# Attention with a mixture of depths: the column of router scores by a diagonal select, in four of eight batches

## The chip, the cores and the metric

The kernel runs on one core of one Trainium2 chip. The metric is the device time of one launch in microseconds. Before the change the median of 3 runs is 205.4 us (205.3 to 205.61). PE is TensorE, DVE is VectorE, ACT is ScalarE, POOL is GpSimd and SP is SyncE.

## The reference

Squared-ReLU attention over 8 batches of 12 heads (448 tokens, 64 columns a head), and then in each batch the 128 tokens with the highest router score go through a two-layer MLP.

```python
# attention, batch 8, heads 12, seq 448, head_dim 64
scores = scale * np.matmul(q, k.transpose(0, 1, 3, 2))
attn = np.maximum(scores, 0.0) ** 2 / S
attn_out = np.matmul(attn, v)
x = attn_out.transpose(0, 2, 1, 3).reshape(B, S, H * D)          # 8 x 448 x 768
# mixture of depths, F = 1024, capacity 128
scores = np.einsum('bsd,d->bs', x, w_gate)
out = x.copy()
for b in range(B):
    top_idx = np.argpartition(-scores[b], capacity)[:capacity]
    xe = x[b, top_idx]
    h = np.maximum(xe @ w1, 0.0)
    ye = h @ w2
    g = 1.0 / (1.0 + np.exp(-scores[b, top_idx]))
    out[b, top_idx] = x[b, top_idx] + g[:, None] * ye
```

## The kernel before

The order of all work is written out by hand: one string of items, `ORDER`, is walked from front to back, and each item issues its instructions. Every engine takes its own instructions in that order and waits only for semaphores. An item is a name and numbers, then the PSUM bank (`at`) and, for an eviction, the engine (`A` for ACT, `D` for DVE). There are 8 PSUM banks, and items share them by number.

Attention goes by units of 4 heads: unit u belongs to batch u // 3, so there are 24. `T` and `TE` transpose q and k on PE and copy them to `qkt` (line 279 on DVE). `S,u,c` makes a block of scores of key group c (0 to 6) in two banks (line 247), `R,u,c` evicts it with a ReLU into `r_sb` (line 275 on ACT, 277 on DVE), `Q,u,g` squares a group of such blocks on DVE into `a_sb` (line 260). The groups are c = 0, 1; c = 2, 3; c = 4, 5, 6. `V,u,c` multiplies block c with v (line 268), so `V,u,2` waits for `Q,u,1`. `X` evicts the result as xT, and `RT`, `RE` turn it into rows of tokens, `x_sb`.

The router follows a batch's last unit. `G` makes the row of scores on PE, with the gate vector spread over all 128 columns, so that every partition of the bank holds the same row of 448 scores. `bc` copies this to `bc_sb` (128 x 512 fp32, line 275 on ACT). The same scores are also needed as a column, one per partition, in 4 groups of 128 tokens: `col` (line 343) makes it by four fp32 PE transposes of partition 0's row with a 1 x 1 identity, into a bank, and `colE` (line 349, DVE) copies the 128 x 4 result into `x_sb` beside the tokens (`cols`). `rk` (line 359, DVE) compares row and column, into the 0/1 tile `mk` and partial ranks; `cs` adds `mk` up on PE, `ri` (line 382, DVE) makes ranks. `sc` scatters token rows by rank to DRAM (line 386, issued from POOL), `rb` reads the first 128 back as `xe` (SP). Then `ix`, `xt` and `xtE` (xeT), `h` and `hE` (first layer), `y` and `yE` (second layer, `orow`), and `ADD` (line 514, POOL) writes them back.

POOL also issues every load of q, k, v and the weights (`Lq`, `Lk`, `Lv`, `W1`, `W2`: lines 108 to 124) and every store of plain rows (`ST`, line 313). `mk` and `bc_sb` have two buffers each, by the parity of the batch. `tie` is a constant mask made by POOL selects near the start (line 180).

Of the kernel before, what the change touches and what calls it, by code (L numbers as in the profile page):

```python
# [23 lines left out]
def kernel(  # L24
# [559 lines left out]
    S,18,5,0 S,17,5,2 R,18,5,0,A yE,2,1,4 y,2,0,2,5 R,17,5,2,A y,2,0,4,5 y,2,0,6,5 sc,3,1 S,17,6,0 col,4,4  # L584
    V,15,0,6 S,18,0,2 ST,2,1 V,15,1,6 V,15,2,6 R,17,6,0,A yE,2,0,5 Q,17,0 V,15,3,6 S,19,0,0 V,15,4,6 sc,3,0
    colE,4,4 R,18,0,2,A sc,3,2 V,15,5,6 V,15,6,6 S,18,2,2 V,17,0,4 R,19,0,0,A V,17,1,4 V,17,2,4 X,15,6,A
    V,17,3,4 Q,17,2 S,18,1,0 V,17,4,4 R,18,2,2,D V,17,5,4 V,17,6,4 V,16,0,6 V,16,1,6 R,18,1,0,A ST,2,0 V,16,2,6
    X,17,4,A S,18,3,2 Lv,6,0,6 V,16,3,6 S,18,4,0 R,18,3,2,A V,16,4,6 ADD,2 V,16,5,6 V,16,6,6 rk,4,0 rk,4,1
    rk,4,3 Lq,7,0,6 R,18,4,0,D T,20,4,0 Lk,7,0,6 X,16,6,A rb,3 T,20,4,1 S,18,6,2 S,19,6,0 rk,4,2 G,5,0,6
    R,18,6,2,A G,5,1,6 TE,20,4,2,D G,5,2,6 R,19,6,0,A xt,3,4 S,19,1,2 ST,3,1 Q,18,0 S,19,5,0 bc,5,6,A R,19,1,2,A  # L590
    ix,3 xtE,3,4,D Q,18,2 RT,17,5 R,19,5,0,A cs,4,4 RT,16,6 ri,4,4 RE,16,6,A col,5,7 S,19,4,2 S,19,2,0 Q,19,0
    R,19,2,0,A h,3,0,4 h,3,1,4 h,3,2,4 colE,5,7 V,18,0,6 Q,18,1 S,19,3,0 R,19,4,2,A V,18,1,6 RE,17,5,D V,18,2,6
    V,18,3,6 S,20,5,2 R,19,3,0,A V,18,4,6 rk,5,0 V,18,5,6 V,18,6,6 R,20,5,2,A S,20,0,0 R,20,0,0,A h,3,3,4
    h,3,4,5 hE,3,0,4,A Q,19,2 h,3,5,5 h,3,6,5 sc,4,2 S,20,4,0 rk,5,3 S,20,3,2 y,3,1,0,4 X,18,6,A Q,19,1 h,3,7,5
    T,21,6,0 T,21,6,1 R,20,4,0,A R,20,3,2,D hE,3,1,5,A S,20,2,0 S,20,1,2 y,3,1,2,4 TE,21,6,2,D sc,4,1 RT,15,5
    sig,3 R,20,2,0,A V,19,0,6 S,21,4,0 V,19,1,6 R,20,1,2,A rk,5,2 V,19,2,6 sc,4,0 V,19,3,6 rk,5,1 V,19,4,6
    RE,15,5,D sc,4,3 V,19,5,6 R,21,4,0,A V,19,6,6 X,19,6,A S,20,6,2 S,21,1,0 ST,4,1 cs,5,5 Q,20,1 y,3,1,4,4
    ri,5,5 ST,3,0 T,22,6,0 T,22,6,1 R,21,1,0,A Q,20,0 R,20,6,2,A S,21,6,0 R,21,6,0,A y,3,0,0,5 TE,22,6,2,D
    y,3,1,6,4 y,3,0,2,5 Q,20,2 y,3,0,4,5 S,22,0,2 S,21,0,0 V,20,0,6 R,22,0,2,A V,20,1,6 V,20,2,6 yE,3,1,4
    R,21,0,0,A V,20,3,6 V,20,4,6 rb,4 V,20,5,6 S,21,2,2 R,21,2,2,A Lv,7,0,6 V,20,6,6 sc,5,2 RT,18,4 y,3,0,6,5  # L600
    X,20,6,D yE,3,0,5 S,21,3,0 Q,21,0 S,22,6,2 T,23,6,0 RE,18,4,A T,23,6,1 sc,5,0 G,6,0,5 R,21,3,0,A G,6,1,5
    R,22,6,2,A G,6,2,5 xt,4,4 bc,6,5,A TE,23,6,2,D S,22,1,2 S,22,2,0 col,6,5 ix,4 xtE,4,4,D h,4,4,7 colE,6,5
    RT,20,4 R,22,1,2,A rk,6,1 h,4,5,7 R,22,2,0,A rk,6,2 rk,6,0 RT,19,5 sig,4 sc,5,1 S,22,3,2 RE,20,4,A RE,19,5,D
    S,21,5,0 h,4,6,7 rk,6,3 h,4,7,7 cs,6,4 sc,5,3 R,21,5,0,A h,4,0,5 h,4,1,5 hE,4,1,7,A R,22,3,2,A Q,21,1
    h,4,2,5 h,4,3,5 ADD,3 S,22,4,0 S,23,2,2 V,21,0,6 hE,4,0,5,A V,21,1,6 ri,6,4 R,23,2,2,A V,21,2,6 Q,21,2
    V,21,3,6 V,21,4,6 V,21,5,6 V,21,6,6 R,22,4,0,D S,22,5,0 R,22,5,0,A S,23,3,2 R,23,3,2,A Q,22,1 y,4,1,0,4
    y,4,1,2,4 y,4,0,0,5 Q,22,0 y,4,1,4,4 X,21,6,A y,4,1,6,4 S,23,4,0 R,23,4,0,A S,23,0,2 ST,4,0 y,4,0,2,5 Zl
    y,4,0,4,5 rb,5 y,4,0,6,5 RT,21,6 xt,5,7 Q,22,2 S,23,1,0 sc,6,0 R,23,0,2,A S,23,5,2 sc,6,3 yE,4,1,4 yE,4,0,5
    RE,21,6,D V,22,0,4 V,22,1,4 ix,5 xtE,5,7,D V,22,2,4 V,22,3,4 Q,23,1 V,22,4,4 V,22,5,4 R,23,1,0,A sc,6,2
    V,22,6,4 S,23,6,0 h,5,4,7 R,23,5,2,A sc,6,1 h,5,0,6 R,23,6,0,A h,5,1,6 Q,23,0 h,5,2,6 h,5,3,6 X,22,4,A  # L610
    h,5,5,7 V,23,0,2 Q,23,2 V,23,1,2 hE,5,0,6,D V,23,2,2 V,23,3,2 V,23,4,2 V,23,5,2 V,23,6,2 ADD,4 G,7,0,6
    RT,22,5 h,5,6,7 G,7,1,6 ST,6,0 X,23,2,A RE,22,5,A G,7,2,6 bc,7,6,A h,5,7,7 RT,23,1 ST,6,1 y,5,0,0,4
    hE,5,1,7,A RE,23,1,A col,7,6 y,5,0,2,4 rb,6 colE,7,6 rk,7,0 y,5,1,0,6 y,5,1,2,6 y,5,1,4,6 y,5,0,4,4
    y,5,0,6,4 rk,7,1 hot,7,1 hot,7,0 y,5,1,6,6 xt,6,7 rk,7,3 sig,5 xg,7,0,0 xg,7,1,0 rk,7,2 hot,7,2 hot,7,3
    xg,7,2,0 xg,7,3,0 ix,6 xtE,6,7,A h,6,0,5 ST,5,0 xgE,7,1,0,A yE,5,1,6 yE,5,0,4 h,6,1,5 h,6,2,5 h,6,3,5
    h,6,4,2 xgE,7,0,0,A h,6,5,2 hE,6,0,5,A p,7,0 p,7,1 h,6,6,2 p,7,2 p,7,3 sel,7,7 ST,5,1 ST,7,0,0,512
    ST,7,1,0,512 ST,7,0,512,768 ST,7,1,512,768 h,6,7,2 sE,7,0,7 sE,7,1,-1 sE,7,2,-1 sgl,7 y,6,1,0,0 y,6,1,2,0
# [56 lines left out]
```

## Time and profile before

| | |
|---|---|
| median of 3 runs | 205.4 us (205.3 to 205.61) |
| the profiled execution's own time | 204.92 us |
| its span, first to last instruction | 203.2 us |
| granted TensorE clock, mean | 0.999 |
| busy: PE, PE weight loads | 188.6 us (93%), 120.9 us (59%) |
| busy: DVE, ACT, POOL | 173.2 us (85%), 166.6 us (82%), 108.9 us (54%) |

Three engines are near full at the same time. A busy share is a mean over the launch, so it doesn't say which of the three sets the pace in a stretch; that is read from the idle time in front of an instruction and from what ended it. Starts are in microseconds from the span's start, and two rows of one engine overlap a little: the distance between two starts is what an instruction takes of its engine, the duration includes its tail.

### The profile page before, as it was taken

Reading aid. Unit: us, or ns where it says so; the run is one execution under the profiler, and the core shown is the slowest. Engines: PE = TensorE matmul, PEld = TensorE weight load, DVE = VectorE, ACT = ScalarE, POOL = GpSimd, SP = SyncE. Lnnn points to the kernel's source line nnn. Section 1 sums busy time; section 2 is a strip of 40 time slices with the busy share of each in tenths; the row PEclk is TensorE's granted clock in tenths of the full one; section 3 lists DMA queues with packets and bytes.
Section 4 is the critical chain, followed back from the end, with each engine's and each line's share of the span. In section 5 each row is a group of like instructions: output and inputs, shape, how many; then the busy total and the mean of one; then the engine's idle time right before and its main releaser. Section 6 shows DMA issues by size and latency. Waiting matters only on the chain.

```text
span 203.2 us, 6985 instructions
## 1 busy us (share of the span) xinstructions
PE 188.6 (93%) x3028; PEld 120.9 (59%) x3028; DVE 173.2 (85%) x274; ACT 166.6 (82%) x216; POOL 108.9 (54%) x133
## 2 busy tenths in 40 slices
...
GB/s 185 180 203 202 205 204 204 206 214 121 16 92 220 206 211 151 280 219 230 52 338 203 125 65 221 222 231 183 210 301 175 130 162 18 75 391 412 175 65 155
DMA packets 28970, 37.89 MB, mean 186 GB/s; under 512 B 2523, under 2 KB 23813, under 8 KB 28940
## 3 DMA queue, kind: packets, MB, share of 16 engines
...
q8 instruction: 23, 0.38, 0.7%
...
## 4 chain that ended last, share of the span: by engine, by line
PE 60%; ACT 25%; issue 6%; DVE 4%; DMA 2%; POOL 1%; POOLq 1%; ACTq 0%; DVEq 0%
PE banks L215 34%; ACT r_sb L275 23%; PE banks L247 14%; PE banks L268 11%; DMA kf<-in_k_dram 2%; ACT xT_sb L275 2%; DVE mk L359 1%; PE banks L343 1%; POOLq L669 1%; DVE qkt L279 1%; DVE a_sb L260 1%; PE banks L154 1%; POOL q_sb L478 1%; POOL out_dram L514 0%; ACT bc_sb L275 0%
## 5 line engine op out<-in xcount | busy, mean ns | idle before, releaser
L275 ACT ACTIVATE r_sb<-banks 128x896 bf16<-128x896 f32 x155 | 132.9, 950 | 12.1 <-PE banks L247 9.4
L260 DVE TENSOR_TENSOR a_sb<-r_sb 128x1792 bf16<-128x1792 bf16 (+1 forms) x72 | 87.4, 1238 | 0.3 <-ACT r_sb L275 0.2
L386 POOL DMA_INDIRECT xe_dram<-x_sb,rank_i x28 | 41.4, 1478 | 51.5 <-DVE rank_i L382 37.8
L247 PE MATMUL banks<-qkt 64*64 64x448 bf16 x672 | 58.4, 363 | 6.5 <-ACT r_sb L275 4.8
L268 PE MATMUL banks<-a_sb,v_sb 64*64 64x448 bf16 x672 | 43.6, 351 | 0.0
L247 PEld LDWEIGHTS <-qkt 64*64 64x64 bf16 x672 | 22.6, 104 | 29.6 <-issue 18.3
L279 DVE COPY qkt<-banks 128x1792 bf16<-128x1792 bf16 (+1 forms) x25 | 26.2, 1050 | 4.8 <-PE banks L215 3.4
L268 PEld LDWEIGHTS <-v_sb 64*64 64x64 bf16 x672 | 21.1, 106 | 9.5 <-issue 1.2
L215 PE MATMUL banks<-xeT,w_sb 128*128 128x128 bf16 x384 | 25.4, 219 | 0.5 <-DVE xeT L279 0.5
L514 POOL DMA_INDIRECT out_dram<-orow,idx x7 | 10.8, 1540 | 27.0 <-DVE orow L509 16.3
L215 PE MATMUL banks<-w_sb,hT 128*128 128x384 bf16 x128 | 24.6, 327 | 0.2 <-DVE hT L277 0.2
L215 PEld LDWEIGHTS <-w_sb 128*128 128x128 bf16 x384 | 22.0, 98 | 4.0 <-issue 3.4
L275 ACT ACTIVATE xT_sb<-banks 128x896 bf16<-128x896 f32 x19 | 18.0, 948 | 2.4 <-PE banks L268 2.4
L277 DVE TENSOR_SCALAR r_sb<-banks 128x896 bf16<-128x896 f32 x13 | 14.1, 1088 | 3.8 <-PE banks L247 2.4
L215 PEld LDWEIGHTS <-hT 128*128 128x128 bf16 x128 | 10.9, 98 | 10.3 <-issue 3.6
L359 DVE SCALAR_TENSOR_TENSOR mk<-bc_sb,x_sb,tie 128x448 bf16<-128x448 f32 (+4 forms) x32 | 15.2, 501 | 0.2
L215 PE MATMUL banks<-ident,xT_sb 128*128 128x128 bf16 x192 | 14.8, 220 | 0.2 <-ACT xT_sb L275 0.2
L215 PE MATMUL banks<-ident,k_sb 128*64 128x128 bf16 x336 | 14.0, 221 | 0.2 <-ACT k_sb L275 0.2
L215 PE MATMUL banks<-ident,q_sb 128*64 128x128 bf16 x336 | 14.0, 222 | 0.1
L215 PEld LDWEIGHTS <-xT_sb 128*128 128x128 bf16 x192 | 11.4, 98 | 4.2 <-issue 2.5
L215 PEld LDWEIGHTS <-q_sb 128*64 128x64 bf16 x336 | 10.3, 109 | 5.8 <-issue 5.0
L313 POOL DMA_DIRECT2D out_dram<-x_sb x18 | 12.1, 679 | 2.1 <-ACT x_sb L275 1.4
...
## 6 DMA issues: line engine op xcount, KB each, us to landing
...
```

The lines of the kernel that those rows point to most:

```text
L154: nc.tensor.matmul(out=banks[col:col + 64, at + x, :S], lhsT=zero[lo:lo + 64, 0:64], rhs=zero[lo:lo + 64, :], start=True, stop=True, skip_ ...
L215: nc.tensor.matmul(out=out, lhsT=lhsT, rhs=rhs, start=start, stop=stop, skip_group_check=True, **kw)
L247: nc.tensor.matmul(out=banks[col:col + 64, at + x, :S], lhsT=sb[lo:lo + 64, 1, c, hh, :], rhs=sb[lo:lo + 64, 0, :, hh, :], start=True, sto ...
L260: nc.vector.tensor_tensor(out=a, in0=r, in1=r, op=ALU.mult)
L268: nc.tensor.matmul(out=banks[col:col + 64, at + x, :S], lhsT=vs[lo:lo + 64, 2 * i + x, c, :], rhs=a[lo:lo + 64, c - SLOTS[g][0], x, :], st ...
L275: nc.scalar.activation(out=out_, in_=in_, func=func or AF.Copy, scale=scale)
L277: nc.vector.tensor_scalar(out=out_, in0=in_, scalar1=0.0, scalar2=None, op0=ALU.max)
L279: nc.vector.tensor_copy(out=out_, in_=in_)
L313: nc.gpsimd.dma_start(out=rows, in_=x_rows[b % NROW][64 * cp:64 * cp + 64, 0:NJ - cp, c0:c1])
L359: nc.vector.scalar_tensor_tensor(out=dst, in0=self.bc_[:n, t0:S], scalar=self.cols[:n, j:j + 1], in1=tie[:n, j, t0:], op0=ALU.subtract, op ...
L386: done = nc.gpsimd.indirect_dma_start(out=xe_dram[self.b][:, :], out_offset=bass.IndirectOffsetOnAxis(ap=self.rank_i[:, j:j + 1], axis=0), ...
L514: done = nc.gpsimd.indirect_dma_start(out=out[0:self.b + 1].rearrange("b s d -> (b s) d"), out_offset=bass.IndirectOffsetOnAxis(ap=self.id ...
```

## The change

In batches 2, 3, 4 and 5, `col` and `colE` give way to `dg` and `dgE`; batches 0, 1, 6 and 7 keep them. `dg` is one POOL select that reads all of `bc_sb` as 4 blocks of 128, keeps in each block the element whose place equals the partition's number, and writes zero elsewhere: 128 x 512 fp32 into the memory of the batch's `mk` tile, which `rk` overwrites afterwards. `dgE` is a DVE sum over each block of 128, which leaves the column in `cols`. No PSUM bank is used. `dg` stands behind `bc` (in batch 4 later, behind the loads `Lv,6`), `dgE` where `colE` stood (in batch 4 later, in front of the first `rk`).

```diff
+        def dg(self):
+            self.own_ = f32(mk_sb[self.b % 2])[:, :NJ * 128].rearrange("p (j t) -> p j t", j=NJ)
+            nc.gpsimd.affine_select(
+                out=self.own_, in_=self.bc_.rearrange("p (j t) -> p j t", j=NJ),
+                compare_op=ALU.is_equal, fill=0.0, base=0, pattern=[[0, NJ], [-1, 128]],
+                channel_multiplier=1)
+
+        def dgE(self):
+            nc.vector.tensor_reduce(out=self.cols, in_=self.own_, axis=mybir.AxisListType.X,
+                                    op=ALU.add)
...
-    S,10,5,2 rk,1,3 bc,2,5,A R,10,5,2,A T,11,6,0 xt,0,5 R,10,2,0,A T,11,6,1 RE,7,4,D rk,1,1 ix,0 xtE,0,5,D
+    S,10,5,2 rk,1,3 bc,2,5,A dg,2 R,10,5,2,A T,11,6,0 xt,0,5 R,10,2,0,A T,11,6,1 RE,7,4,D rk,1,1 ix,0 xtE,0,5,D
...
```

DVE in batches 3 to 4, from the second-layer evictions of batch 2 to the `TE` of unit 20; `x_sb_93` holds the column of batch 4, `a_sb` rows are `Q`. Before:

```order
L509 SCALAR_TENSOR_TENSOR orow<-banks,g__2503,xe 128x384 x2
L260 TENSOR_TENSOR a_sb_2718<-r_sb_2624 128x1792
L349 COPY x_sb_93<-banks 128x4
L260 TENSOR_TENSOR a_sb_2772<-r_sb_2567 128x2688
L277 TENSOR_SCALAR r_sb_2782<-banks 128x896
L359 SCALAR_TENSOR_TENSOR mk_97,rank_f_99<-bc_sb_95,x_sb_93,tie 128x448
```

And now:

```order
L521 SCALAR_TENSOR_TENSOR orow<-banks,g__2497,xe 128x384 x2
L260 TENSOR_TENSOR a_sb_2708<-r_sb_2618 128x1792
L260 TENSOR_TENSOR a_sb_2761<-r_sb_2561 128x2688
L277 TENSOR_SCALAR r_sb_2771<-banks 128x896
L357 TENSOR_REDUCE x_sb_93<-mk_97 128x4
L371 SCALAR_TENSOR_TENSOR mk_97,rank_f_99<-bc_sb_95,x_sb_93,tie 128x448
```

The column moves two instructions back, behind `Q,17,2` and `R,18,2`, and reads `mk` instead of a bank.

DVE in batch 5, from xeT to the square `Q,18,1` (`a_sb_2985`, now `a_sb_2973`) and what follows it. Before:

```order
L279 COPY xeT<-banks 128x768
L260 TENSOR_TENSOR a_sb_2917<-r_sb_2677 128x2688
L382 TENSOR_TENSOR rank_i<-rank_f_99,banks 128x4
L260 TENSOR_TENSOR a_sb_2958<-r_sb_2757 128x1792
L349 COPY x_sb_94<-banks 128x4
L260 TENSOR_TENSOR a_sb_2985<-r_sb_2782 128x1792
L279 COPY x_sb_94<-banks 128x4x256
```

And now:

```order
L279 COPY xeT<-banks 128x768
L260 TENSOR_TENSOR a_sb_2909<-r_sb_2671 128x2688
L394 TENSOR_TENSOR rank_i<-rank_f_99,banks 128x4
L260 TENSOR_TENSOR a_sb_2946<-r_sb_2746 128x1792
L357 TENSOR_REDUCE x_sb_94<-mk_98 128x4
L260 TENSOR_TENSOR a_sb_2973<-r_sb_2771 128x1792
L279 COPY x_sb_94<-banks 128x4x256
```

Here the sum stands exactly where the copy stood, directly in front of `Q,18,1`.

POOL in batch 2, from the loads of k and v to the scatters of batch 1 and the stores behind them; `w_sb` is the load `W2`. Before:

```order
L111 DMA k_sb_85<-in_k_dram 128x6x448
L115 DMA v_sb_87<-in_v_dram 128x3x448
L118 DMA v_sb_87<-in_v_dram 64x3x448 x2
L124 DMA w_sb<-in_moe_w_dram 128x8x768
L386 DMA xe_dram_103<-x_sb_93,rank_i 128x386 x4
```

And now:

```order
L111 DMA k_sb_85<-in_k_dram 128x6x448
L115 DMA v_sb_87<-in_v_dram 128x3x448
L118 DMA v_sb_87<-in_v_dram 64x3x448 x2
L351 AFFINE_SELECT mk_97<-bc_sb_95 128x512
L124 DMA w_sb<-in_moe_w_dram 128x8x768
L398 DMA xe_dram_103<-x_sb_93,rank_i 128x386 x4
```

The select stands in front of `W2`, whose issue is therefore behind `bc,2`.

## Rows read from the trace of the kernel before

**Rows 1.** The page's first part: busy us, share of the span, instructions.

```profile
PE 188.6 (93%) x3028; PEld 120.9 (59%) x3028; DVE 173.2 (85%) x274; ACT 166.6 (82%) x216; POOL 108.9 (54%) x133
```

**Rows 2.** The page's chain that ended last, by engine, share of the span.

```profile
PE 60%; ACT 25%; issue 6%; DVE 4%; DMA 2%; POOL 1%; POOLq 1%; ACTq 0%; DVEq 0%
```

**Rows 3.** The chain in order of time at `col,2`: start, us, what.

```profile
72.73 0.34 PE banks L343 x4
```

**Rows 4.** Timelines of ACT and DVE, batch 2: start, us, what, idle before, releaser.

```profile
70.11 4.40 ACT L275 ACTIVATE r_sb<-banks 128x896 bf16<-128x896 f32 x5
75.00 3.35 ACT L275 ACTIVATE r_sb<-banks 128x896 bf16<-128x896 f32 x4 [0.49 <-ACT r_sb L275]
...
79.42 1.09 DVE L277 TENSOR_SCALAR r_sb<-banks 128x896 bf16<-128x896 f32 x1 [1.04 <-PE banks L215]
```

**Rows 5.** Timeline of all engines, batch 3.

```profile
92.52 0.55 ACT L275 ACTIVATE bc_sb<-banks 128x448 f32<-128x448 f32 x1
...
94.96 0.49 PE L215 MATMUL banks<-xeT,w_sb 128*128 128x128 bf16 x6 [0.51 <-DVE xeT L279]
...
98.26 0.92 ACT L275 ACTIVATE r_sb<-banks 128x896 bf16<-128x896 f32 x1 [1.52 <-PE banks L247]
...
99.18 1.09 DVE L277 TENSOR_SCALAR r_sb<-banks 128x896 bf16<-128x896 f32 x1 [1.14 <-PE banks L247]
```

**Rows 6.** DVE's timeline through batches 4 and 5.

```profile
127.32 1.09 DVE L279 COPY qkt<-banks 128x1792 bf16<-128x1792 bf16 x1 [0.36 <-PE banks L215]
...
130.50 0.16 DVE L349 COPY x_sb<-banks 128x4 f32<-128x4 f32 x1
130.57 1.55 DVE L260 TENSOR_TENSOR a_sb<-r_sb 128x2688 bf16<-128x2688 bf16 x1
132.04 1.08 DVE L277 TENSOR_SCALAR r_sb<-banks 128x896 bf16<-128x896 f32 x1
133.04 0.68 DVE L359 SCALAR_TENSOR_TENSOR mk<-bc_sb,x_sb,tie 128x448 bf16<-128x448 f32 x1
...
133.64 0.55 DVE L359 SCALAR_TENSOR_TENSOR mk<-bc_sb,x_sb,tie 128x320 bf16<-128x320 f32 x1
...
140.90 1.08 DVE L260 TENSOR_TENSOR a_sb<-r_sb 128x1792 bf16<-128x1792 bf16 x1
141.90 0.69 DVE L279 COPY x_sb<-banks 128x1024 bf16<-128x1024 bf16 x1
```

**Rows 7.** Timeline of PE's weight loads at `V,18,2`.

```profile
142.04 0.14 PEld L268 LDWEIGHTS <-v_sb 64*64 64x64 bf16 x7 [0.15 <-issue]
```

**Rows 8.** Timeline around `W2`: ACT's `bc,2`, POOL's `W2`, PE's first `y`.

```profile
60.15 0.97 POOL L124 DMA_DIRECT2D w_sb<-in_moe_w_dram x1
...
67.82 0.54 ACT L275 ACTIVATE bc_sb<-banks 128x448 f32<-128x448 f32 x1
...
83.39 1.47 PE L215 MATMUL banks<-w_sb,hT 128*128 128x384 bf16 x8
```

**Rows 9.** Stretches: us, busy by engine, clock, DMA share, GB/s.

```profile
62.00:64.00 2.00, 1.92 (x44) 1.18 (x39) 2.00 (x3) 2.00 (x3) 0.00 (x0) 1.00 1.23 231
...
78.00:80.00 2.00, 2.00 (x37) 1.53 (x36) 0.96 (x2) 2.00 (x4) 1.93 (x3) 1.00 0.19 62
```

**Rows 10.** POOL's selects of `tie` at line 180: duration min/median/max in ns.

```profile
L180 POOL TENSOR_SCALAR_AFFINE_SELECT tie<-tie x4: 553/1062/1417, 20.7 to 28.4; 128x448 bf16<-128x448 bf16 x4
```

**Rows 11.** DVE and POOL at the longest of these selects, timelines of each.

```profile
23.11 2.08 DVE L260 TENSOR_TENSOR a_sb<-r_sb 128x1792 bf16<-128x1792 bf16 x2
24.19 1.42 POOL L180 TENSOR_SCALAR_AFFINE_SELECT tie<-tie 128x448 bf16<-128x448 bf16 x1
```

**Rows 12.** POOL's and ACT's timeline in front of the selects of batches 4 and 5.

```profile
127.81 1.31 POOL L118 DMA_DIRECT2D v_sb<-in_v_dram x2
...
137.62 0.55 ACT L275 ACTIVATE bc_sb<-banks 128x448 f32<-128x448 f32 x1
```

More of the change, by code (lines that the diff above doesn't have):

```diff
@@ L566 @@
     S,13,6,0 T,14,6,0 X,11,4,A T,14,6,1 R,13,6,0,D cs,2,4 R,13,5,2,A S,12,0,0 Lv,4,0,6 TE,14,6,2,D Q,12,2 ADD,0
-    S,12,1,2 R,12,0,0,A rb,1 R,12,1,2,A G,3,0,5 G,3,1,5 G,3,2,5 xt,1,6 Q,12,0 S,14,3,0 bc,3,5,A ri,2,4 S,13,0,2
-    sc,2,3 RT,11,5 sig,1 sc,2,1 col,3,7 ix,1 xtE,1,6,D R,14,3,0,A S,14,2,0 R,13,0,2,A h,1,4,4 colE,3,7 rk,3,0
+    S,12,1,2 R,12,0,0,A rb,1 R,12,1,2,A G,3,0,5 G,3,1,5 G,3,2,5 xt,1,6 Q,12,0 S,14,3,0 bc,3,5,A dg,3 ri,2,4
+    S,13,0,2 sc,2,3 RT,11,5 sig,1 sc,2,1 ix,1 xtE,1,6,D R,14,3,0,A S,14,2,0 R,13,0,2,A h,1,4,4 dgE,3 rk,3,0
     S,13,3,2 R,14,2,0,A RT,10,6 rk,3,3 sc,2,2 R,13,3,2,A S,13,4,0 R,13,4,0,A h,1,5,4 RE,11,5,D h,1,0,5 h,1,6,4
@@ L583 @@
     R,17,1,0,A y,2,1,2,4 T,19,6,0 Q,17,1 R,17,0,2,A y,2,0,0,5 y,2,1,4,4 Q,16,2 y,2,1,6,4 T,19,6,1 TE,19,6,2,D
[L584 to L617, printed above, removed]
@@ L618 @@
-    ADD,5 xr,7 hE,6,1,2,D y,6,1,4,0 y,6,1,6,0 sig,6 h,7,0,4 h,7,4,1 yE,6,1,0 h,7,5,1 h,7,1,4 h,7,2,4 h,7,3,4
-    h,7,6,1 h,7,7,1 hE,7,0,4,D hE,7,1,1,A y,6,0,0,6 y,6,0,2,6 y,6,0,4,6 y,6,0,6,6 yE,6,0,6 ADD,6 y,7,1,0,2
-    y,7,0,0,4 y,7,0,2,4 y,7,1,2,2 y,7,0,4,4 y,7,0,6,4 y,7,1,4,2 yE,7,0,4 y,7,1,6,2 yE,7,1,2 ADD,7
+    S,18,5,0 S,17,5,2 R,18,5,0,A yE,2,1,4 y,2,0,2,5 R,17,5,2,A y,2,0,4,5 y,2,0,6,5 sc,3,1 S,17,6,0 V,15,0,6
+    S,18,0,2 ST,2,1 V,15,1,6 V,15,2,6 R,17,6,0,A yE,2,0,5 Q,17,0 V,15,3,6 S,19,0,0 V,15,4,6 sc,3,0 R,18,0,2,A
@@ new lines @@
+    sc,3,2 V,15,5,6 V,15,6,6 S,18,2,2 V,17,0,4 R,19,0,0,A V,17,1,4 V,17,2,4 X,15,6,A V,17,3,4 Q,17,2 S,18,1,0
+    V,17,4,4 R,18,2,2,D V,17,5,4 V,17,6,4 V,16,0,6 V,16,1,6 R,18,1,0,A ST,2,0 V,16,2,6 X,17,4,A S,18,3,2
+    Lv,6,0,6 dg,4 V,16,3,6 S,18,4,0 R,18,3,2,A V,16,4,6 ADD,2 V,16,5,6 V,16,6,6 dgE,4 rk,4,0 rk,4,1 rk,4,3
+    Lq,7,0,6 R,18,4,0,D T,20,4,0 Lk,7,0,6 X,16,6,A rb,3 T,20,4,1 S,18,6,2 S,19,6,0 rk,4,2 G,5,0,6 R,18,6,2,A
+    G,5,1,6 TE,20,4,2,D G,5,2,6 R,19,6,0,A xt,3,4 S,19,1,2 ST,3,1 Q,18,0 S,19,5,0 bc,5,6,A dg,5 R,19,1,2,A ix,3
@@ new lines @@
+    xtE,3,4,D Q,18,2 RT,17,5 R,19,5,0,A cs,4,4 RT,16,6 ri,4,4 RE,16,6,A S,19,4,2 S,19,2,0 Q,19,0 R,19,2,0,A
+    h,3,0,4 h,3,1,4 h,3,2,4 dgE,5 V,18,0,6 Q,18,1 S,19,3,0 R,19,4,2,A V,18,1,6 RE,17,5,D V,18,2,6 V,18,3,6
+    S,20,5,2 R,19,3,0,A V,18,4,6 rk,5,0 V,18,5,6 V,18,6,6 R,20,5,2,A S,20,0,0 R,20,0,0,A h,3,3,4 h,3,4,5
+    hE,3,0,4,A Q,19,2 h,3,5,5 h,3,6,5 sc,4,2 S,20,4,0 rk,5,3 S,20,3,2 y,3,1,0,4 X,18,6,A Q,19,1 h,3,7,5 T,21,6,0
+    T,21,6,1 R,20,4,0,A R,20,3,2,D hE,3,1,5,A S,20,2,0 S,20,1,2 y,3,1,2,4 TE,21,6,2,D sc,4,1 RT,15,5 sig,3
```

31 lines of the change are left out of this document (28 added, 3 removed).

## The prediction

> **What bounds the kernel now.** I read the busy shares first, then the chain of waits, then the timelines at the four places that the change touches. The shares alone decide nothing: PE has 188.6 us of work in a span of 203.2 us, but DVE has 173.2 us [rows 1], and DVE is idle at the start and the end, so in the middle it can be as full as PE. The chain puts 60% of the span on PE and only 4% on DVE [rows 2]. By this view the change takes work from the engine that sets the end and gives work to two that don't. The reader should keep in mind what a chain can't show: it names the engine that came last, and not by how little the next one came earlier. That margin is read from the idle time in front of instructions, place by place.
>
> Two places have idle time on DVE, and one has none. Behind batch 2's column DVE waits 1.04 us for PE at 79.42 us [rows 4]. Behind batch 3's it waits 1.14 us at 99.18 us, and ACT 1.52 us at 98.26 us [rows 5]. In batches 4 and 5 DVE works without a gap worth naming from 127.32 to 141.90 us [rows 6]; the wait in front of 127.32 us was for PE. In this stretch DVE is a full queue, started by PE and then running by itself.
>
> **What goes.** Each of the four changed columns takes four fp32 transposes off PE, 0.34 us a column in the chain in order of time [rows 3]; batches 4 and 5 have a piece as long there, and batch 3's transposes stand inside a wait. Four columns make 4 x 0.34 = 1.36 us of PE, which is the most that the change can give back. It also takes four copies off DVE. They last 0.16 us, but the next instruction starts 0.07 us after them (130.50 to 130.57 us) [rows 6], so DVE gets back 0.07 us each.
>
> **What comes on DVE.** The trace has no fp32 sum over blocks, so it is bounded by what DVE does to fp32 elsewhere. The nearest row is the comparison of 128 x 448: the next one starts 0.60 us after it (133.04 to 133.64 us), and the comparison of 320 lasts 0.13 us less, 1.0 ns an element [rows 6]. 64 elements more make 0.67 us. The eviction of 128 x 896 fp32 takes 1.00 us (132.04 to 133.04 us) [rows 6], which for 512 elements is 0.57 us. I take 0.61 us, between the two. As ends I keep 0.35 us, should DVE do two of these elements in the time of one, and 0.85 us, should a sum run a quarter slower than the comparison. At 0.61 us each column adds 0.61 - 0.07 = 0.54 us to DVE.
>
> [...]
>
> **What comes on POOL.** A select of 128 x 448 bf16 takes 0.553 to 1.417 us [rows 10]. For 512 elements that makes 0.63 to 1.62 us; if fp32 goes at half the pace, 3.24 us. I take 1.2 us, near the median. What hides it is POOL's idle time and the distance to the sum:
> - Batch 2: `bc` ends at 68.36 us [rows 8], and the copy that the sum replaces came behind the transposes, at 73.07 us [rows 3]. Even 3.24 us is hidden.
> - Batch 3: `bc` ends at 93.07 us [rows 5], and the sum falls due just after the xeT copy that PE waits for at 94.96 us. 1.2 us is just in time, 1.62 us is at the edge, 3.24 us would hold DVE some 1.4 us, most of which its own 1.14 us of idle time behind takes.
> - Batch 4: POOL is free behind `Lv,6` at 129.12 us [rows 12], the sum has moved behind `R,18,2` and falls due at 133 us. Hidden.
> - Batch 5: `bc` ends at 138.17 us [rows 12], the sum stands in front of the square that started at 140.90 us [rows 6]. Hidden, but for the largest value.
>
> **What is queued behind the select.** In batch 2 POOL meets `W2` only behind the select: 60.15 us becomes some 69.6 us [rows 8]. The load is 1024 x 768 numbers, 1.5 MB as bf16; the DMA engines moved 231 GB/s when full and had nearly run dry at 78 to 80 us (share 0.19) [rows 9], so `W2` had landed by then. Starting 9.5 us later it finds the queues nearly empty and needs 6.8 us at that rate: 77 us, or some 81 us if the scatters and a slower start cost it 4 us. PE first reads it at 83.39 us [rows 8]. I cost this at nothing; the cover is 2 to 6 us.
>
> **Place by place, on the path.**
> - Batch 2. PE reaches the next scores 0.34 us earlier, but ACT is in a row of five evictions without a gap from 70.11 to 74.51 us [rows 4], 0.86 us apart, and the bank that these scores need is free after the third, at about 72.7 us. So 0.3 us of the 0.34 pass, and they are kept if ACT's gap of 0.49 us in front of 75.00 us shrinks. DVE is 0.54 us later from here, which its 1.04 us of idle time at 79.42 us takes [rows 4]. Taken: 0.3 us gained, with 0 and 0.34 as ends.
> - Batch 3. PE waits 0.51 us for xeT here, and DVE makes xeT before the column [rows 5]. The transposes stood inside this wait: without them the wait is 0.34 us longer. Nothing is gained. The 0.54 us on DVE goes into the 1.14 us at 99.18 us. Taken: 0.
> - Batches 4 and 5. DVE's full stretch now holds two more sums and two copies fewer, 2 x 0.54 = 1.08 us, in front of the square `Q,18,1` that ended at 141.90 us [rows 6]. `V,18,2` reads this square. Its first weight load stood at 142.04 us after an idle 0.15 us [rows 7]: PE and DVE arrived together, with at most 0.14 us to spare. With the change PE arrives 2 x 0.34 us earlier, DVE 1.08 us later, and PE waits. PE goes on 1.08 - 0.14 = 0.94 us later than before. From there to the end the work is fed by PE again, and the delay stays.
>
> The sum is -0.3 + 0 + 0.94 = 0.64 us. Against the profiled execution's 204.92 us that is 205.56 us; the median of the three runs lies 0.48 us above that execution, so as a time that compares with the median: 205.4 + 0.64 = 206.0 us. With the lower end of the sum on DVE (0.35 us) the last term is 2 x 0.28 - 0.14 = 0.42 us and the time 205.5 us; with the upper (0.85 us) it is 1.42 us, and without the gain of batch 2 the time is 206.8 us.
>
> **Rivals.**
> 1. *PE is the bound throughout, and DVE's margin is wider than I read it.* For it: 60% against 4% of the chain [rows 2]. Against it: DVE's stretch without a gap up to a consumer that waits [rows 6, 7]. It would be decided by `V,18,2`: if DVE could be a microsecond later there, all columns but batch 3's come through, 3 x 0.34 = 1.0 us, 204.4 us; with batch 3's, 204.0 us.
> 2. *The delay at 142 us is given back or eaten.* Gaps on several engines at once, as at 98 to 99 us [rows 5], are not explained by any one engine's work. If there is such slack behind 142 us too, the excess of DVE ends in it: 205.4 us, give or take 0.4.
> 3. *The select holds DVE.* Select and squares read SBUF at the same time in batches 3 to 5. If a square waited for the select, by the select's 0.63 to 1.62 us in each of batches 4 and 5, the time would be 206.0 + 1.3 = 207.3 us to 206.0 + 3.2 = 209.2 us. Against it: beside a select of 1.42 us, where the shortest took 0.553 us, two squares took 2.08 us [rows 10, 11], no more than the 1.08 us each that `Q,18,1` takes [rows 6]. It is the select that stretches, and DVE doesn't pay. [...] A late `W2` has the same sign and goes with this rival.
>
> **How the numbers follow.** My forecast 0.48, with its own range 205.5 to 206.8 us; rival 1 0.24, rival 2 0.23, rival 3 0.05. What a measurement here can tell from no change is 0.2%, 0.41 us. Of the forecast 0.38 is slower by more than that and 0.10 within it; of rival 1 0.22 is faster and 0.02 within; of rival 2 0.04 faster, 0.15 within and 0.04 slower; rival 3 is slower. That makes faster 0.26, within 0.27, slower 0.47. The range 204.2 to 206.9 us leaves out the best end of rival 1 and all of rival 3.
>
> **What would show it.** In the changed kernel's profile: PE has 16 matmuls fewer; DVE has four sums of about 0.6 us, and from about 127 to 143 us still no gap; the weight load of `V,18,2` has an idle time of about 1.5 us in front of it, ended by DVE's square; `W2` is issued at about 70 us and PE doesn't wait for it. The forecast is wrong if there is no wait for a square there, if the sum takes under 0.35 us, or if DVE has idle time inside that stretch.

## The result, and the profile after

| | before | changed |
|---|---|---|
| median of 14 runs each, one chip | 205.66 us (205.06 to 206.44) | 206.86 us (205.72 to 207.45) |
| ratio, 95% interval | | 1.0056 (1.0040 to 1.0072) |
| profiled execution: time, span | 204.92 us, 203.2 us | 207.03 us, 205.3 us |

The kernel became slower, by 1.15 us (0.8 to 1.5). The forecast was 206.0 us, +0.64 us. The measured 206.86 us lies just above the forecast's own range (205.5 to 206.8 us) and within the range over all rivals (204.2 to 206.9 us); the kernel before had itself moved, from 205.4 to 205.66 us.

The two profiled executions lie 2.11 us apart. Of this, 1.04 us is there at 58 us, in front of the first changed instruction. So the traces are compared from 60 us on, by how much later the same instruction starts: +1.04 us in front of the change, +2.11 at the end, net +1.07. A second profile of the changed kernel (after_again, from a later group of runs) against the same one of before goes from +0.87 to +1.95, net +1.08. On the way:

| stretch | profile after | second profile | forecast |
|---|---|---|---|
| batches 2 and 3 (60 to 100 us) | -0.60 | -0.61 | -0.3 |
| batches 4 and 5 (127 to 146 us) | +0.98 | +0.96 | +0.94 |
| a pause at 177 us | +0.68 | +0.73 | 0 |

The page's first part, columns as in [rows 1]:

```profile
PE 188.0 (92%) x3012; PEld 120.2 (59%) x3012; DVE 177.0 (86%) x274; ACT 167.1 (81%) x216; POOL 112.7 (55%) x137
```

PE has 16 matmuls and 0.6 us less, DVE 3.8 us more, POOL four selects more. The chain by engine, against [rows 2]:

```profile
PE 40%; DVE 23%; DMA 12%; issue 10%; ACT 8%; POOL 5%; POOLq 1%; DVEq 0%; ACTq 0%
```

DVE has gone from 4% to 23%, though the time grew by half a per cent: the chain names who came last, and a small delay turns long pieces of it over. (DMA's 12% are three loads of q that it now passes through.) Where it matters it runs through the new sum. The chain in order of time at batch 5:

```profile
142.15 0.60 DVE x_sb L357
142.75 1.01 DVE a_sb L260
143.80 0.57 PE banks L268 x8
```

The sum of batch 5, the square `Q,18,1`, then `V,18,2` on PE. DVE's timeline of the same stretch, against [rows 6]:

```profile
127.76 1.09 DVE L279 COPY qkt<-banks 128x1792 bf16<-128x1792 bf16 x1 [0.34 <-PE banks L215]
...
129.94 2.70 DVE L260 TENSOR_TENSOR a_sb<-r_sb 128x1792 bf16<-128x1792 bf16 x2
...
133.56 0.67 DVE L357 TENSOR_REDUCE x_sb<-mk 128x4 f32<-128x512 f32 x1
134.27 0.68 DVE L371 SCALAR_TENSOR_TENSOR mk<-bc_sb,x_sb,tie 128x448 bf16<-128x448 f32 x1
...
139.43 1.65 DVE L260 TENSOR_TENSOR a_sb<-r_sb 128x2688 bf16<-128x2688 bf16 x1
...
142.07 0.67 DVE L357 TENSOR_REDUCE x_sb<-mk 128x4 f32<-128x512 f32 x1
142.67 1.07 DVE L260 TENSOR_TENSOR a_sb<-r_sb 128x1792 bf16<-128x1792 bf16 x1
143.67 0.68 DVE L279 COPY x_sb<-banks 128x1024 bf16<-128x1024 bf16 x1
```

DVE works without a gap worth naming. From one start to the next the sums take 0.71 us, where the comparison that reads the sum is next, and 0.60 us, where a square is next (forecast 0.61). DVE enters 0.44 us later than before (127.76 against 127.32) and leaves `Q,18,1` 1.77 us later (143.67 against 141.90). PE's weight loads, against [rows 7]:

```profile
143.80 0.14 PEld L268 LDWEIGHTS <-v_sb 64*64 64x64 bf16 x7 [0.98 <-issue]
```

The idle time of 0.15 us has become 0.98 us. The prediction expected about 1.5 us, with PE early. PE is not early, since it had to wait for DVE once already, behind batch 4's sum (PE's timeline; no wait there before):

```profile
136.69 0.38 PE L247 MATMUL banks<-qkt 64*64 64x448 bf16 x4 [0.32 <-DVE r_sb L277]
```

At `V,18,2` PE is 1.76 us later, 1.32 us more than in front of the stretch. Some 0.3 us of that is given back a microsecond on, because the kernel before waits there itself. PE's timeline of the kernel before:

```profile
145.27 0.57 PE L247 MATMUL banks<-qkt 64*64 64x448 bf16 x8 [0.23 <-issue]
```

and of the changed one, where the same matmuls start 1.42 us later without a wait:

```profile
146.69 0.57 PE L247 MATMUL banks<-qkt 64*64 64x448 bf16 x8
```

Batch 2 in the timeline of all engines, against [rows 4]:

```profile
71.15 5.20 ACT L275 ACTIVATE r_sb<-banks 128x896 bf16<-128x896 f32 x6
...
74.58 0.67 DVE L357 TENSOR_REDUCE x_sb<-mk 128x4 f32<-128x512 f32 x1
...
75.17 1.54 DVE L260 TENSOR_TENSOR a_sb<-r_sb 128x2688 bf16<-128x2688 bf16 x1
...
76.81 2.54 ACT L275 ACTIVATE r_sb<-banks 128x896 bf16<-128x896 f32 x3 [0.45 <-DVE a_sb L260]
...
79.92 1.08 DVE L277 TENSOR_SCALAR r_sb<-banks 128x896 bf16<-128x896 f32 x1
```

DVE's idle time of 1.04 us is gone; by the forecast 0.50 us of it would be left. And ACT now waits 0.45 us for the square at 75.17 us, `Q,9,2`, in front of which the sum stands. Batch 3 in the same view, against [rows 5]: PE's wait for xeT has grown from 0.51 to 0.93 us, ACT's idle time of 1.52 us is 0.76 us, and DVE's of 1.14 us is gone, where the forecast would leave 0.60 us.

```profile
96.16 0.49 PE L215 MATMUL banks<-xeT,w_sb 128*128 128x128 bf16 x6 [0.93 <-DVE xeT L279]
...
98.70 0.92 ACT L275 ACTIVATE r_sb<-banks 128x896 bf16<-128x896 f32 x1 [0.76 <-PE banks L247]
99.70 1.08 DVE L277 TENSOR_SCALAR r_sb<-banks 128x896 bf16<-128x896 f32 x1
```

The forecast had the wait for xeT 0.34 us longer, by the transposes taken out in front of it. It grew for another reason. The time of the transposes has become a wait for ACT, in front of the scores that come before xeT (PE's timeline):

```profile
94.85 0.38 PE L247 MATMUL banks<-qkt 64*64 64x448 bf16 x4 [0.34 <-ACT r_sb L275]
```

And xeT itself is late. DVE's two squares in front of it took 2.55 us before:

```profile
91.76 2.55 DVE L260 TENSOR_TENSOR a_sb<-r_sb 128x2688 bf16<-128x2688 bf16 x2
```

and take 3.00 us now, while POOL's select runs (the experiments below show that it is the cause):

```profile
92.51 3.00 DVE L260 TENSOR_TENSOR a_sb<-r_sb 128x2688 bf16<-128x2688 bf16 x2
```

By the starts of the same PE instructions, batch 2 goes from +1.04 to +0.78 us. Batch 3 first loses 0.66 us: 0.42 at xeT, and 0.24 where PE needs a bank that DVE empties behind the sum. Then 1.00 us is gained at once, at 99 us, where PE waited 1.17 us for ACT before and now waits 0.17 us. So the -0.60 us of the table is a loss in batch 3 under a pause that is no longer there.

The forecast says nothing of the table's last line. ACT's timeline at 177 us, where the wait was 0.36 us before and is 1.06 us now:

```profile
175.41 0.92 ACT L275 ACTIVATE r_sb<-banks 128x896 bf16<-128x896 f32 x1 [0.36 <-PE banks L247]
```

```profile
177.51 0.92 ACT L275 ACTIVATE r_sb<-banks 128x896 bf16<-128x896 f32 x1 [1.06 <-PE banks L247]
```

POOL's timeline: the selects, and `W2` behind the first, against [rows 8] and [rows 10].

```profile
69.47 0.64 POOL L351 TENSOR_SCALAR_AFFINE_SELECT mk<-bc_sb 128x512 f32<-128x512 f32 x1 [7.94 <-ACT bc_sb L275]
70.07 0.95 POOL L124 DMA_DIRECT2D w_sb<-in_moe_w_dram  x1
...
93.93 0.64 POOL L351 TENSOR_SCALAR_AFFINE_SELECT mk<-bc_sb 128x512 f32<-128x512 f32 x1 [2.76 <-ACT bc_sb L275]
...
129.51 0.70 POOL L351 TENSOR_SCALAR_AFFINE_SELECT mk<-bc_sb 128x512 f32<-128x512 f32 x1
...
139.03 0.63 POOL L351 TENSOR_SCALAR_AFFINE_SELECT mk<-bc_sb 128x512 f32<-128x512 f32 x1 [3.08 <-ACT bc_sb L275]
```

The selects take 0.63 to 0.70 us, the low end of the range (1.2 us was taken). `W2` is issued at 70.07 us (forecast 69.6; this profile runs 1.04 us late here), and PE's first `y` starts at 84.17 us without a wait.

### The profile page after: what moved, and what is told of

The parts are those of the page before. It is cut to its first block, busy times and chain, and to the rows that moved or that the text cites. A ratio compares the mean times of both kernels' runs of the same rounds, so it can differ in the third digit from the quotient of the medians.

```text
span 205.3 us, 6954 instructions
## 1 busy us (share of the span) xinstructions
PE 188.0 (92%) x3012; PEld 120.2 (59%) x3012; DVE 177.0 (86%) x274; ACT 167.1 (81%) x216; POOL 112.7 (55%) x137
## 4 chain that ended last, share of the span: by engine, by line
PE 40%; DVE 23%; DMA 12%; issue 10%; ACT 8%; POOL 5%; POOLq 1%; DVEq 0%; ACTq 0%
PE banks L215 23%; DMA q_sb<-in_q_dram 12%; DVE a_sb L260 12%; PE banks L247 10%; ACT r_sb L275 7%; PE banks L268 7%; DVE qkt L279 3%; DVE mk L371 2%; POOL xe_dram L398 2%; DVE x_sb L279 2%; DVE xT_sb L281 2%; POOL out_dram L526 1%; DVE r_sb L277 1%; POOLq L681 1%; POOL out_dram L313 1%
## 5 line engine op out<-in xcount | busy, mean ns | idle before, releaser
L260 DVE TENSOR_TENSOR a_sb<-r_sb 128x1792 bf16<-128x1792 bf16 (+1 forms) x72 | 89.2, 1263 | 1.0 <-ACT r_sb L275 0.9
L247 PE MATMUL banks<-qkt 64*64 64x448 bf16 x672 | 59.0, 363 | 6.4 <-ACT r_sb L275 3.9
L398 POOL DMA_INDIRECT xe_dram<-x_sb,rank_i x28 | 43.8, 1566 | 37.8 <-DVE rank_i L394 27.5
L268 PE MATMUL banks<-a_sb,v_sb 64*64 64x448 bf16 x672 | 44.3, 351 | 1.6 <-DVE a_sb L260 1.4
L268 PEld LDWEIGHTS <-v_sb 64*64 64x64 bf16 x672 | 21.8, 106 | 11.3 <-issue 3.5
L526 POOL DMA_INDIRECT out_dram<-orow,idx x7 | 9.8, 1405 | 24.0 <-DVE orow L521 13.3
```

The source lines that it names most:

```text
L247: nc.tensor.matmul(out=banks[col:col + 64, at + x, :S], lhsT=sb[lo:lo + 64, 1, c, hh, :], rhs=sb[lo:lo + 64, 0, :, hh, :], start=True, sto ...
L260: nc.vector.tensor_tensor(out=a, in0=r, in1=r, op=ALU.mult)
L268: nc.tensor.matmul(out=banks[col:col + 64, at + x, :S], lhsT=vs[lo:lo + 64, 2 * i + x, c, :], rhs=a[lo:lo + 64, c - SLOTS[g][0], x, :], st ...
L398: done = nc.gpsimd.indirect_dma_start(out=xe_dram[self.b][:, :], out_offset=bass.IndirectOffsetOnAxis(ap=self.rank_i[:, j:j + 1], axis=0), ...
L526: done = nc.gpsimd.indirect_dma_start(out=out[0:self.b + 1].rearrange("b s d -> (b s) d"), out_offset=bass.IndirectOffsetOnAxis(ap=self.id ...
```

## The experiments

They ran in three groups, each on another chip and beside runs of the kernel before on that chip, 6 to 12 runs of each changed kernel. With the first comparison, whose chip is not on record, these are four groups, and in them the kernel before took 205.7, 201.1, 205.2 and 201.0 us. So only differences of times inside a group are compared. The text speaks of the chips of 205 us and those of 201 us. All figures are differences to before, in us, with a 95% interval.

**Which batch, and how (before 201.1 us).** The first two split the change: batches 4 and 5 alone, batches 2 and 3 alone, the others with the transposes as before.

```diff
 only45: batch 2's (batch 3's alike)
-... bc,2,5,A dg,2 ...   h,0,0,5 TE,12,6,2,D dgE,2 Q,9,2
+... bc,2,5,A ...   col,2,4 ...   h,0,0,5 TE,12,6,2,D colE,2,4 Q,9,2
 only23: batch 5's (batch 4's alike)
-h,3,2,4 dgE,5 V,18,0,6 Q,18,1
+col,5,7 ...   h,3,2,4 colE,5,7 V,18,0,6 Q,18,1
```

> The changed kernel with the columns of batches 2 and 3 back on TensorE; only batches 4 and 5 have the select and the sum. Theory A (the two sums lie in VectorE's full queue in front of the square that the second half of V,18 reads): +0.9 to +1.1 us against the kernel before, about 206.7 us, with VectorE's square ending the idle time in front of V,18,2 (about 0.8 us more than before). Rival B (the loss comes from batches 2 and 3, where W2 is issued 9.9 us later and a select stretched two squares by 0.45 us): within 0.3 us of the kernel before.

> The changed kernel with the columns of batches 4 and 5 back on TensorE; only batches 2 and 3 have the select and the sum. Theory A: faster than the kernel before by 0.3 to 0.6 us, about 205.2 us; VectorE is later by one sum behind batch 2 and again behind batch 3, and both times its idle time (1.04 and 1.14 us before) takes it. Rival B (late W2, stretched squares): slower by 0.5 to 1.1 us.

Measured: only45 +1.21 (0.76 to 1.65), only23 +0.68 (0.36 to 1.01). Both halves cost here. The next two work on DVE's stretch: the sums of batches 4 and 5 twice, and batch 5's sum moved behind the square that PE waits for.

```diff
 twice45
-dgE,4 rk,4,0 ...   dgE,5 V,18,0,6 Q,18,1
+dgE,4 dgE,4 rk,4,0 ...   dgE,5 dgE,5 V,18,0,6 Q,18,1
 sum5_behind
-h,3,2,4 dgE,5 V,18,0,6 Q,18,1 S,19,3,0
+h,3,2,4 V,18,0,6 Q,18,1 dgE,5 S,19,3,0
```

> The changed kernel with the sums of batches 4 and 5 made twice (the second one writes the same four numbers). Theory A: two more sums of 0.60 us in the full queue, so V,18,2 starts 1.2 us later than in the changed kernel and the time is 206.9 + 1.2 = 208.1 us. Rival C (slack behind V,18,2 takes part of a delay, or the loss has to do with the select and not with the sum): +0 to +0.5 us.

> The changed kernel with the sum of batch 5 behind the square Q,18,1 instead of in front of it; nothing else moves. Theory A: the square ends 0.60 us earlier, V,18,2 waits 0.6 us less, and the time is 206.9 - 0.6 = 206.3 us; VectorE has the same work and the comparison behind it starts when it did. Rival C (the loss is the select's, the rank's or a DMA's): no change, 206.9 us.

Measured: twice45 +3.54 (3.06 to 4.02), sum5_behind +1.61 (1.09 to 2.13). The same weight load of `V,18,2` on PE's queue, first in only45:

```profile
140.39 0.14 PEld L268 LDWEIGHTS <-v_sb 64*64 64x64 bf16 x7 [0.92 <-issue]
```

in twice45:

```profile
143.03 0.14 PEld L268 LDWEIGHTS <-v_sb 64*64 64x64 bf16 x7 [1.71 <-issue]
```

and in sum5_behind:

```profile
140.52 0.14 PEld L268 LDWEIGHTS <-v_sb 64*64 64x64 bf16 x7 [0.39 <-issue]
```

In only23, which has no sum there, the idle time is gone. From 125 us of only23 to just behind `V,18,2` (143 us), by the starts of the same PE instructions, only45 loses 1.17 us against only23, sum5_behind 0.56 (one sum less: 0.61), and twice45 2.60 (two more: +1.43). So what stands on DVE in front of `Q,18,1` goes into PE's time nearly one for one, 0.6 to 0.7 us a sum. This is the forecast's mechanism, and rival 1 (PE the bound) and rival 2 (given back) fall for this stretch: only45 keeps its 1.17 us to the end. sum5_behind loses 0.22 us again at 146 us, so moving the sum saved 0.39 us there. Its time (+1.61) and the sum of the two halves (0.68 + 1.21) can't be told apart.

For batch 2, ACT's timeline in only23:

```profile
75.97 2.54 ACT L275 ACTIVATE r_sb<-banks 128x896 bf16<-128x896 f32 x3 [0.45 <-DVE a_sb L260]
```

and the timeline of all engines in only45, where batch 2 is as before:

```profile
69.79 7.66 ACT L275 ACTIVATE r_sb<-banks 128x896 bf16<-128x896 f32 x9
...
78.06 1.09 DVE L277 TENSOR_SCALAR r_sb<-banks 128x896 bf16<-128x896 f32 x1
```

Nine evictions without a gap, and no idle time on DVE: the 1.04 us of [rows 4] that the forecast used as cover is not there on this chip. With the sum ACT waits 0.45 us, and PE is 0.48 us later behind it.

**Does moving the sum mend it, and what does a select alone cost (before 205.2 us).** after_again is the changed kernel once more. select_only is the kernel before plus the four selects, which nothing reads. sum2_behind has batches 2 and 3 changed and batch 2's sum behind `Q,9,2`. two_and_five_behind has batches 2 and 5 changed, both sums behind their squares, by the edits of sum2_behind and sum5_behind.

```diff
 select_only, from before (batches 3 to 5 alike, batch 4 behind Lv,6)
-bc,2,5,A R,10,5,2,A
+bc,2,5,A dg,2 R,10,5,2,A
 sum2_behind, from only23
-TE,12,6,2,D dgE,2 Q,9,2 rk,2,2
+TE,12,6,2,D Q,9,2 dgE,2 rk,2,2
```

> The changed kernel itself, once more, so that it stands beside the runs of this call. If the parts add up (batches 2 and 3 cost 0.6 us of 201 in the earlier call, batches 4 and 5 cost 1.1), it is 1.5 to 2.0 us slower than the kernel before; the first comparison, in which batches 2 and 3 seemed to cost nothing, gave 1.15 us. A chip whose stalls swallow the delay of batches 2 and 3 gives 1.1 again.

> The kernel before with the four selects on GpSimd added and nothing else: the columns come from TensorE as before and the sums are left out, so what the selects write is not read. Theory A (the sum on VectorE is the cost): within 0.2 us of the kernel before, although W2 is issued behind the select of batch 2, some 9 us later. Rival B (a select that shares memory with VectorE's squares holds them, or W2 comes late): slower by 0.4 to 1.0 us.

> Selects and sums in batches 2 and 3 alone, as in an earlier run that was 0.6 us slower than the kernel before, but with the sum of batch 2 behind the square Q,9,2 instead of in front of it. Theory A (that square frees the buffer which ScalarE's eviction at 76 us waited 0.45 us for): the wait goes and the time is 0.1 to 0.3 us above the kernel before, what batch 3 costs. Rival D (the loss is batch 3's, or late DMAs'): no change, 0.6 us above.

> Selects and sums in batches 2 and 5 alone, each sum behind the square that it delayed (Q,9,2 and Q,18,1); batches 3 and 4 have their columns by TensorE. Theory A (only the place of the sums cost time): TensorE's two pieces of 0.34 us are gained where it is not waiting, 0.3 to 0.7 us faster than the kernel before. Rival E (a sum behind the square delays the next square as much, and VectorE is as full there): no change to 0.4 us slower.

Measured: after_again +0.92 (0.39 to 1.46), select_only +0.94 (0.53 to 1.35), sum2_behind +0.27 (-0.23 to 0.76), two_and_five_behind +2.05 (1.29 to 2.81). sum2_behind can't be told from before. The surprise is select_only: selects that nobody waits for cost as much as the whole change. Its profile, against before from 60 us on, shows where: PE loses 0.42 us in batch 3, at xeT, and 0.49 us in batches 4 and 5, the most of it at `V,18,2`. At the first `y`, which reads the late `W2`, it loses nothing. (0.28 us more is lost at 62 us, in front of the first select.) PE's timeline at xeT, with the transposes still in place, and PE's weight load of `V,18,2` (idle 0.15 us before):

```profile
95.63 0.49 PE L215 MATMUL banks<-xeT,w_sb 128*128 128x128 bf16 x6 [0.93 <-DVE xeT L279]
```

```profile
143.19 0.14 PEld L268 LDWEIGHTS <-v_sb 64*64 64x64 bf16 x7 [0.47 <-issue]
```

Its timeline of all engines at batch 5:

```profile
138.95 0.63 POOL L351 TENSOR_SCALAR_AFFINE_SELECT mk<-bc_sb 128x512 f32<-128x512 f32 x1 [2.70 <-ACT bc_sb L275]
...
139.00 2.00 DVE L260 TENSOR_TENSOR a_sb<-r_sb 128x2688 bf16<-128x2688 bf16 x1
```

The square of 2688 takes 1.55 us without a select [rows 6], here 2.00. It started 0.05 us behind the select and paid 0.45 us of the 0.58 that the select still had to go. Where the square is first it is the other way round; the timeline of only23 at batch 3:

```profile
91.28 2.55 DVE L260 TENSOR_TENSOR a_sb<-r_sb 128x2688 bf16<-128x2688 bf16 x2
...
93.09 1.24 POOL L351 TENSOR_SCALAR_AFFINE_SELECT mk<-bc_sb 128x512 f32<-128x512 f32 x1 [2.76 <-ACT bc_sb L275]
```

Two squares in 2.55 us, unstretched. The select starts 0.34 us behind the second one, and its row lasts 1.24 us instead of 0.64. In the profile after the select starts at 93.93 us, 0.05 us ahead of the second square, and the same pair takes 0.45 us more (3.00 us, shown above). So in both cases the one that started first ran on and the other took longer, and in batch 3 some 0.4 us in the select's start decide whether PE's xeT is late: it is in the profiles of after, after_again, select_only and sum2_behind, and isn't in only23 and after_16_more. In batch 5 of the profile after the square shown above took 1.65 us, 0.10 more than before: it began 0.40 us behind the select of 139.03 us, which had 0.23 us to go. In batch 4 the two squares at 129.94 us took 2.70 us, 0.15 more than such a pair without a select; they began with 0.28 us of the select of 129.51 us to go. Copies from the banks beside a select are not longer: in the profile after xeT takes 0.54 us beside the select of 139.03 us and `x_sb` 0.68 beside that of 69.47 us, in before 0.55 and 0.68. A comparison of 128 x 320 that began with 0.40 us of the select of 69.47 us to go took 0.75 us, 0.21 more than in before. So DVE paid less than the select had to go, on the squares by 0.13 us (0.58 less 0.45; 0.23 less 0.10; 0.28 less 0.15) and on the comparison by 0.19 us. How the two engines hold each other, the traces don't show.

two_and_five_behind shows something else. PE's timeline:

```profile
135.75 1.02 PE L247 MATMUL banks<-qkt 64*64 64x448 bf16 x8
```

Eight matmuls in 1.02 us, where eight of this kind take 0.57 at 145 us: a pause of 0.45 us inside a group of four, with no wait. Another follows, where before waits 0.23 us:

```profile
146.81 0.57 PE L247 MATMUL banks<-qkt 64*64 64x448 bf16 x8 [1.00 <-issue]
```

Together they are 1.2 us of the +2.05. So this run doesn't tell what moving batch 5's sum is worth.

**Parts alone, and the 177 us pause (before 201.0 us).** The pause at 177 us is in both profiles of the changed kernel, and in no other kernel's on the chips of 205 us. One theory was that it goes with the position in PE's instruction stream, from which the change takes 16 matmuls. before_16_fewer takes 16 matmuls out of the warm-up of the kernel before, after_16_more puts 16 short ones into that of the changed kernel. sum_only is before plus four sums over the broadcast itself, into a tile that nobody reads, without selects. two_alone changes batch 2 only, its sum behind the square.

```diff
 before_16_fewer
-for i in range(n):
+for i in range(n - 16):
 (each of them 240 columns wide in place of 128)
 after_16_more
-for i in range(n):
+for i in range(n + 16):
+    w = 128 if i < n - 16 else 64
 sum_only: batch 2's, from before (3 to 5 alike; tensor_reduce of the broadcast into a spare tile)
-colE,2,4 Q,9,2
+colE,2,4 dgE,2 Q,9,2
 two_alone: batch 2's, from the changed kernel (3 to 5 as before)
-TE,12,6,2,D dgE,2 Q,9,2 rk,2,2
+TE,12,6,2,D Q,9,2 dgE,2 rk,2,2
```

> The kernel before with 20 warm-up matmuls of 240 columns at its start in place of 36 of 128, while TensorE waits for its first data: the later TensorE instructions are the same, but as in the changed kernel there are 16 matmuls and 16 weight loads fewer in all. Two profiles of the changed kernel have 1.06 and 1.11 us of idle time on ScalarE at 177 us, behind a TensorE result that was over a microsecond old, and no profile of another kernel has it. Theory F (it comes from where TensorE's instructions lie in its stream): that idle time appears here and the time is 0.3 to 0.7 us longer. Rival G (it follows from the order and times of the work): it doesn't appear, no change.

> The changed kernel with 52 warm-up matmuls, 32 of them of half the size, in place of 36, so that TensorE has as many instructions as in the kernel before. Theory F: the idle time at 177 us goes, and 0.3 to 0.7 us of the change's 1.1 us with it. Rival G: it stays, and the time is 0.9 to 1.2 us above the kernel before.

> The kernel before with four sums on VectorE added at the changed kernel's places, each over the scores row itself into a spare tile that nothing reads; no select, and the columns come from TensorE as before. Theory A: in batches 4 and 5 two sums of 0.60 us less 0.14 us of margin make 1.06 us at V,18,2; in batch 2 the ScalarE eviction waits 0 to 0.45 us for the square behind the sum, in batch 3 0 to 0.26 us: 1.1 to 1.8 us slower than the kernel before. Rival B (the select is the whole cost): within 0.3 us.

> Select and sum in batch 2 alone, the sum behind the square Q,9,2; batches 3 to 5 have their columns by TensorE. Theory A: TensorE's 0.34 us are gained, the select costs VectorE 0.2 us of a comparison that it holds: 0 to 0.3 us faster than the kernel before. Rival E (VectorE or ScalarE set the pace there, or W2's late load does): 0 to 0.5 us slower.

Measured: before_16_fewer +0.10 (-0.34 to 0.56), after_16_more +1.61 (1.02 to 2.19), sum_only +1.73 (1.19 to 2.29), two_alone +0.68 (0.26 to 1.13). On this chip no kernel's profile has the pause, so these numbers neither bear the theory out nor refute it; it stays open. after_16_more is the changed kernel but for its warm-up, so its +1.61 is the best figure for what the change costs on a chip of 201 us. sum_only shows the sums' cost without any select, with the same two waits. ACT in batch 2:

```profile
75.82 2.54 ACT L276 ACTIVATE r_sb<-banks 128x896 bf16<-128x896 f32 x3 [0.44 <-DVE a_sb L261]
```

and PE's weight load of `V,18,2`:

```profile
141.22 0.14 PEld L269 LDWEIGHTS <-v_sb 64*64 64x64 bf16 x7 [0.94 <-issue]
```

two_alone has batch 2's sum behind `Q,9,2`. There ACT waits no more (eight evictions in 6.62 us from 71.88), but the next square is late in its turn, and PE waits for that. The timeline of all engines:

```profile
80.76 1.08 DVE L260 TENSOR_TENSOR a_sb<-r_sb 128x1792 bf16<-128x1792 bf16 x1
...
81.89 0.95 PE L268 MATMUL banks<-a_sb,v_sb 64*64 64x448 bf16 x16
```

This costs PE some 0.3 us. The rest of its +0.68 is in a pause of 0.45 us as above, at the same instruction, on another chip; up to there two_alone and two_and_five_behind are the same kernel:

```profile
134.12 1.02 PE L247 MATMUL banks<-qkt 64*64 64x448 bf16 x8
```

None of the kernels tried is faster than the one before.

Last, where the kernel before itself loses time on a chip of 205 us. Its profile against that of before_16_fewer, which from 60 us on is the same program on a chip of 201 us: it falls back by 4.2 us, most of it in steps of 0.4 us at 76, 0.2 at 82, 0.4 at 95, 1.3 at 99, 0.3 at 145, 1.0 at 155 and 0.2 us at 178. The first four stand beside the idle times of [rows 4, 5], on which the forecast built.

## Why the prediction was right and wrong

**Batches 4 and 5: right, in place and size.** Forecast +0.94, found +0.98 and +0.96 (1.17 in only45, on a chip of 201 us). PE waits at `V,18,2` for the square that stands behind the sums, and three experiments that change the number of sums in front of it (none, one, four) move the wait with them. Within the sum errors cancel. DVE's excess over the stretch was forecast as 1.08 us and is 1.33 (1.77 less 0.44): the selects stretched work on DVE by 0.10 us (batch 5) and 0.15 us (batch 4), which was costed at nothing. The 0.14 us taken off for a spare margin wasn't there, since PE is 1.32 us later at `V,18,2`. And 0.3 us is given back at 145 us, where the forecast let the delay stay; on the chip of 201 us it is 0.04.

**Batch 2: the step that failed.** It says of DVE's 0.54 us that "its 1.04 us of idle time at 79.42 us takes" it, and takes 0.3 us as gained. Between the sum and that idle time stands `Q,9,2`, which frees the buffer that ACT's seventh eviction needs. ACT waits for it, 0.45 us in the profile after, 0.45 in only23, 0.44 in sum_only; on the chips of 201 us PE is 0.47 to 0.49 us later for it. And the idle time is no property of the program: on those chips the kernel has none there. In the profile after, batch 2 reads -0.26 us, near the -0.3 that was forecast, but this is luck: PE loses 0.39 us by ACT's wait, and the kernel before loses 0.44 us at 76 us and 0.19 us at 82 us in steps that the changed one doesn't have.

**Batch 3: 0 was forecast, and it is not one number.** On the chips of 201 us the batch costs 0.27 us: PE waits 0.34 us for ACT where the transposes stood, and a bank that DVE empties behind the sum comes free later. On those of 205 us the same bank costs 0.24 us, and the select, costed at nothing, makes xeT 0.42 us late; the forecast's wait for xeT (0.85 us forecast, 0.93 found) came out near for the wrong reason. The pause of [rows 5], with DVE idle for 1.09 to 1.14 us at 99 us, is in before, select_only and two_and_five_behind, and in none of after, after_again and sum2_behind, which changes this batch's net from +0.66 to -0.34 us. So batches 2 and 3 together read -0.6 us there. What the pause is, the traces don't show; "gaps not explained by any one engine's work", as rival 2 put it, was the right caution, and the wrong thing to set a cost against in batches 2 and 3.

**177 us: not foreseen.** +0.68 and +0.73 us, with ACT waiting 1.06 and 1.11 us for a result of PE that the profile has as over 1 us old. This is more than the whole difference between the forecast's +0.64 and the net +1.07; the -0.6 of batches 2 and 3, where -0.3 was forecast, hides part of it. Cause open.

**Rival 3: thrown out wrongly.** Squares that began beside a running select took 0.10 to 0.45 us longer. The argument against it rested on one case [rows 11], in which the squares ran first, and took it for the rule. Its price was overrated (0.63 to 1.62 us in each of batches 4 and 5; 0.10 to 0.45 was seen on a square), since the select took 0.63 to 0.70 us and the squares paid 0.13 us less than it still had to go. With the selects alone it costs +0.94 us.

**Smaller terms.** The sum: 0.60 us where a square is next, 0.71 and 0.78 where the comparison that reads it is next (batches 4 and 3), forecast 0.61. The select: 0.63 to 0.70 us, forecast 1.2. `W2`: as forecast, no wait. The transposes: 0.6 us off PE's busy time, none of which was seen as gain on the chips of 201 us, where the parts add up to some 1.9 us of loss (0.68 + 1.21; 1.61 measured in one piece, with an interval that takes in 1.9).

In all: the right direction and the right main mechanism. That +0.64 and +1.15 us lie no further apart is partly luck: 0.66 us of loss in batch 3 and 0.68 at 177 us were not foreseen, and a pause of 1.00 us that is gone at 99 us took most of this back.
